# Opening of a fused convolution and SwiGLU kernel: when block 1's x is requested, which queue loads block 0's x, and where pair 1's first group and the third gate bank stand

## The chip, the cores and the metric

The kernel runs on one core of a Trainium2 chip. The metric is device time in microseconds (us), median of several executions. A core has five engines that work side by side, each in its own program order: TensorE (PE, matmuls into PSUM banks), VectorE (DVE), ScalarE (ACT), GpSimd (POOL) and SyncE (SP, which here only issues DMAs and waits). ACT and POOL issue DMAs too. All of them hand their transfers to the same 16 DMA engines.

## The reference

The input x has 8 sequences of 4096 tokens with 192 channels. A causal convolution of 7 taps runs along each sequence; the 192 channels form 8 heads of 24, and the taps are per head, softmaxed over the 7. Its result goes through a SwiGLU feed-forward block with 1536 hidden units.

```
w = softmax(weight)                              # 8 heads x 7 taps
y[b, s, h, :] = sum_k w[h, k] * x_padded[b, s + k, h, :]
g = y @ w_gate;  val = y @ w_val                 # 192 -> 1536
out = (silu(g) * val) @ w_out                    # 1536 -> 192
```

## The kernel before

**Tiling.** The 32768 tokens are cut into 64 blocks of 512 (TB); two blocks make a pair. The 1536 hidden units are cut into 12 chunks of 128 (NCH). The main loop at the end of the kernel runs over blocks and, in each, over chunks; a counter (`at`) numbers the chunks through: 0 to 11 are block 0, 12 to 23 block 1, and chunk 24 begins pair 1. For each chunk PE computes gate and value (`first`, L541 and L542, three steps of two matmuls each, a gate and a value matmul side by side on the two halves of the array), ACT takes silu of the gate (L546), and DVE multiplies it by the value into h (L548). Pieces of the block before's last product (`second`, L553: h times w_out) are put between the chunks from chunk 14 on; ACT evacuates them (L591) and SP stores them (L583).

**PSUM banks.** Two banks hold gates, three hold values, one ("run") belongs to the convolution of the later pairs, and one tile ("acc") to the output. A gate bank is free when silu has read it, a value bank when h is made. In block 0 alone, the chunks named in `PLAN["third"]` take "run" as a third gate bank.

**Convolution of pair 1 and later.** x is loaded by SP in squares of 32 by 32 (`emit_load`, L103, tiles sqA, sqB, and headA, headB for the first pair of a sequence), turned by DVE (`emit_turn`, L114, tiles xtA, xtB), and the taps are split between engines: ACT multiplies tap 0 into "run" (`start_d`, L468) and others into t tiles (L461), DVE adds taps onto "run" (`dve_tap`, L478, the last into aD), POOL multiplies taps (L483), adds the t tiles (L490) and joins all into xc (L496). SP then exchanges the two 64-partition halves into xs (`swapped`, L444 and L445). A pair has three such groups (0, 1, 2; group 1 is the B half). At which chunk each step of a group is put into the program is written by hand in `PLAN`; for pair 1 it is `PLAN["opening"]`, one tuple per group in the order turn, start, ACT taps, DVE taps, POOL taps, join, swap. Steps due at a chunk (`at_chunk`) are put behind that chunk's silu and h.

**Convolution of pair 0.** It is done on PE. `load_x` (L136) brings x of one block into x_sb as six windows of 94 rows. The taps (L132) are turned into a softmaxed band matrix T by small operations on PE, ACT and DVE (L248 to L270), the repeated products (`repeat`, L310) and DVE's cut by a band mask (`cut_band`, L318). For block 0, ACT and POOL cast x to 16 bits (`cast`, L220), PE multiplies by T (`heads`, `convolve`, L331), and the sums are gathered (L380) into the operands D0 to D2. `warm` (L240) are matmuls on zeros that only keep PE occupied. For block 1, POOL casts x by parity into x16p (`cast_parity`, L223), and the product is made between the chunks of block 0: `lateA(0)` behind chunk 2, `lateA(1)` behind chunk 5, `lateC` behind chunk 8. ACT copies the sums (foldA, L660; foldC, L666) and SP exchanges halves (`exchange`, L657: swapA, swapC). Chunk 12 on needs foldA, swapA, foldC and swapC.

**Order of SP's queue before.** Block 0's x (two DMAs); then, behind a wait for block 0's first convolution (`heads(0, 0)`), block 1's x (two DMAs of three windows) and pair 1's sqB; behind `lateA(0)` the first halves of pair 1's sqA; the exchanges for block 1; at chunk 9 the second halves of sqA; group 1's exchange at chunk 13; from then on loads, exchanges, stores and marks (`mark`, L438: an SP no-op that waits for a PE output piece and that a later piece waits for).

**Order of POOL's queue before.** Four iotas, `plain` (L199, L200), the memset of `spread` (L205), the weights of chunks 0 to 3 (`load_w`, L156, a casting DMA each for gate and value), block 0's casts, two copies into `spread` (`place`, L279), the weights of chunks 4 to 7, two more copies, `mask` (L289, L290) and `own` (L297), block 1's casts, the weights of chunks 8 to 11, w_out (L593).

Of the kernel before, what the change touches and what calls it, by code (L numbers as in the profile page):

```python
# [15 lines left out]
    load=((2, -47), (3, -40), (0, -34), (1, -28)),  # L16
    opening=(
# [3 lines left out]
    ),  # L21
    gate=2, val=3, lead=4, third=(2, 8, 11),
)


# [1 line left out]
def kernel(  # L27
# [9 lines left out]
    nc = tc.nc  # L37
    fp32 = mybir.dt.float32
    fp16 = mybir.dt.float16
    int32 = mybir.dt.int32  # L40
    AF = mybir.ActivationFunctionType
    ALU = mybir.AluOpType
    AX = mybir.AxisListType

    B, S, D = x.shape
    H, K = weight.shape
# [4 lines left out]
    grp = D // H  # L51
# [7 lines left out]
    n_pairs = NT // (2 * TB)  # L59
# [3 lines left out]
    const_pool = ctx.enter_context(tc.tile_pool(name="const", bufs=1))  # L63
# [18 lines left out]
    def emit_load(q, part, half=None):  # L82
        head = q % ppb == 0
        if part == 2 and not half:
            squares[q, "A"] = headA if head else xpool.tile(
                [P, HIST + 2 * TB], fp32, tag="sqA", name="sqA"
            )
            squares[q, "B"] = headB if head else xpool.tile(
                [P, HIST + TB], fp32, tag="sqB", name="sqB"
            )  # L90
        for k in range(2):
            quad = 2 * (part % 2) + k
            if part < 2:
                tile_, t0, n, c = squares[q, "A"], 0, 2 * TB, SQ * quad
            else:
                tile_, t0, n, c = squares[q, "B"], TB * (part % 2), TB, P + SQ * k
            skip = HIST if head and t0 == 0 else 0
            row = q * 2 * TB + t0 - HIST + skip
            n = n // SQ + 1 - skip // SQ
            if half is not None:  # L100
                first = TB // SQ + 1
                skip, row, n = ((skip, row, first), (first * SQ, row + first * SQ, n - first))[half]
            nc.sync.dma_start(  # L103
                out=tile_[quad * SQ : (quad + 1) * SQ, skip : skip + n * SQ].rearrange("p (n c) -> p n c", c=SQ),
                in_=x_flat[row : row + n * SQ, c : c + SQ].rearrange("(n p) c -> p n c", p=SQ),
            )
# [9 lines left out]
    def sync_after(ins, earlier, why="one bank, two halves of the array"):  # L116
        tc.add_manual_dep(
            ins.ins,
            earlier.ins.name,
            mybir.DependencyInfo(mybir.DependencyClass.Sync, mybir.DependencyReason.DATA),  # L120
            reason=why,
        )
# [3 lines left out]
    HALF, STEP, W, NW = TB // 2, 85, 88, 6  # L126
# [2 lines left out]
    assert 8 == K + 1 and (NW - 1) * STEP + W > TB and HALF - 3 * STEP in (0, 1)  # L129
    RT = 8 * H  # L130
    taps = const_pool.tile([H, K], fp32, tag="taps", name="taps")
    nc.scalar.dma_start(out=taps, in_=weight)  # L132
    x_sb = xpool.tile([P, 2, NW, D], fp32, tag="x_sb", name="x_sb", bufs=1)

    def load_x(b, lo, hi, skip=0):
        nc.sync.dma_start(  # L136
            out=x_sb[skip:LOADED, b, lo:hi, :],
            in_=bass.AP(
                tensor=x_flat.tensor,
                offset=x_flat.offset + (b * TB + lo * STEP - pad + skip) * D,  # L140
                ap=[[D, LOADED - skip], [STEP * D, hi - lo], [1, D]],
            ),
        )

    load_x(0, 1, NW)
    load_x(0, 0, 1, pad)
    w = wpool.tile([P, 3, Dff], fp16, tag="w_sb", name="w_sb")
    wo_r = wpool.tile([P, NCH, D], fp16, tag="wo_sb", name="wo_sb")
# [5 lines left out]
    def load_w(lo, hi, which):  # L154
        rows, src = w_halves[which]
        nc.gpsimd.dma_start(out=w[rows, :, lo * P : hi * P], in_=src[:, :, lo * P : hi * P])  # L156
# [27 lines left out]
    def where(out, t, bits):  # L184
# [13 lines left out]
    spread = const_pool.tile([P, 4, 2, DB], fp16, tag="spread", name="spread")  # L198
    nc.gpsimd.memset(plain, 0.0)  # L199
    nc.gpsimd.affine_select(  # L200
        out=plain, in_=plain, pattern=[[-32, 4], [-1, grp]],
        compare_op=ALU.not_equal, fill=1.0, base=0, channel_multiplier=1,
    )
    plain = plain[:, :, :].rearrange("p h c -> p (h c)")
    nc.gpsimd.memset(spread, 0.0)  # L205
    load_w(0, 4, 0)
    load_w(0, 4, 1)

    mask = const_pool.tile([RT, D], fp16, tag="mask", name="mask")


    x16 = xpool.tile([P, NW, D + 8], fp16, tag="x16", name="x16", bufs=1)
# [6 lines left out]
    def cast(copy, lo, hi):  # L219
        copy(x16[0:ROWS, lo:hi, 0:D], x_sb[0:ROWS, 0, lo:hi, :])  # L220
# [17 lines left out]
    def warm(n, r=SUBS):  # L238
        for _ in range(n):
            nc.tensor.matmul(  # L240
                early["idle"][:, 0 : r * P].rearrange("p (r c) -> p r c", c=P), zeros,
                zeros.unsqueeze(1).to_broadcast([P, r, P]), start=True, stop=True,
            )

    warm(2)
    warm(1, 3)
    rows = early["D2"][0:RT, 0:K]
    nc.tensor.matmul(rows, whose, taps, start=True, stop=True)  # L248
    nc.vector.tensor_reduce(wmax, rows, axis=AX.X, op=ALU.max, negate=True)
# [20 lines left out]
    nc.vector.tensor_tensor(left[:, 1, :, :], repeated(full), left[:, 0, :, :], op=ALU.subtract)  # L270
    left = left[:, :, :, :].rearrange("r i n m -> r i (n m)")
    nc.scalar.activation(two, one, AF.Silu)
    cast(nc.scalar.copy, 1, 3)
    cast(nc.gpsimd.tensor_copy, 3, NW)
    cast(nc.gpsimd.tensor_copy, 0, 1)

    def place(k):
        lo, hi, at = ((0, DB, 0), (DB, 96, 0), (0, 32, 32), (32, 96, 0))[k]
        nc.gpsimd.tensor_copy(  # L279
            spread[:, k, :, at : at + hi - lo], plain[:, lo:hi].unsqueeze(1).to_broadcast([P, 2, hi - lo])  # L280
        )
# [4 lines left out]
    load_w(4, 8, 1)  # L286
    place(2)
    place(3)
    nc.gpsimd.memset(mask, 0.0)  # L289
    nc.gpsimd.affine_select(  # L290
        out=mask[:, :].rearrange("r (h c) -> r h c", h=H),
        in_=mask[:, :].rearrange("r (h c) -> r h c", h=H),
        pattern=[[-8, H], [0, grp]],
        compare_op=ALU.not_equal, fill=1.0, base=0, channel_multiplier=1,
    )
    own = const_pool.tile([RT, P], fp16, tag="own", name="own")
    nc.gpsimd.tensor_copy(  # L297
        own[:, :].rearrange("h (t c) -> h t c", t=2),
# [9 lines left out]
    def repeat(part, h0):  # L308
        bank = early[("hi", "lo")[part] + "AC"[h0 // HH]]
        return nc.tensor.matmul(  # L310
            bank[0:ROWS, 0 : HH * W], left[:, part, 0:ROWS],
            pick[:, h0 : h0 + HH, :].unsqueeze(2).to_broadcast([RT, HH, W // 8, 8]),
            start=True, stop=True,
        )
# [9 lines left out]
    def convolve(bank, quarters, parts, parities):  # L324

        for part in parts:
            for e in parities:
                for n in range(len(quarters[0])):
                    for a, q in enumerate(quarters):
                        x, h, u0, out = q[n](e)  # L330
                        ins = nc.tensor.matmul(  # L331
                            bank[32 * a : 32 * a + 32, out], x, T[0:ROWS, part, h, u0 : u0 + out.stop - out.start],
                            start=part + e + n == 0, stop=part == 1 and e == parities[-1],
                            skip_group_check=True,
                        )
        return ins

    def piece(win, t0):
        return ends[win] - win * STEP, slice(ends[win] - t0, ends[win + 1] - t0)

    def by_head(h):
        return [
            lambda e, w=w: (x16[0:ROWS, w, grp * h : grp * h + 32], h, *piece(w, 0))
            for w in (3, 4, 5, 0, 1, 2)
        ]

    def by_block(b, half):
# [5 lines left out]
        return [lambda e, w=w: of(e, w) for w in range(half * NW // 2, (half + 1) * NW // 2)]  # L353

    warm(3)
    repeat(0, 0)
    repeat(1, 0)
    repeat(0, HH)
    repeat(1, HH)
# [16 lines left out]
    def heads(k, part):  # L376
        return convolve(sums[k], [by_head(HH * k + a) for a in range(4)], (part,), (0,))
# [3 lines left out]
            early[name], spread[:, k, :, :].rearrange("p t c -> p (t c)"), fold, start=first, stop=last  # L381
        )

    some = heads(0, 0)

    sync_after(nc.sync.nop(), some, "the rest after block 0's x")
    load_x(1, 0, 3)
    load_x(1, 3, NW)
    if n_pairs > 1:
        for part in (2, 3):  # L390
            emit_load(1, part, None)
    heads(0, 1)
    nc.scalar.copy(foldA, sums[0])
    heads(1, 0)
# [13 lines left out]
    raw, rest = (const_pool.tile([RT, K], fp32, tag=n, name=n) for n in ("raw", "rest"))  # L408
# [279 lines left out]
    for q in range(2, n_pairs):  # L688
        base = 2 * NCH * q
        for part, c in PLAN["load"]:  # L690
            c = {2: 14, 3: 16, 0: 18, 1: 21}[part] if q == 2 else base + c
            at_chunk(c, lambda q=q, part=part: emit_load(q, part))
        for g in range(3):
            c = base + PLAN["start"][g]
# [8 lines left out]
    lead = PLAN["lead"]  # L703
# [4 lines left out]
    for n in range(2 * n_pairs):  # L708
        block = Block(n)
# [90 lines left out]
```

## Time and profile before

| | us |
|---|---|
| median of the runs before (lowest to highest) | 778.47 (777.98 to 779.33) |
| the profiled execution | 779.9 |
| its span, first to last instruction | 778.1 |
| PE busy in the span | 766.6 (99%) |
| VectorE, ScalarE, GpSimd busy | 658.5, 662.8, 668.1 |

How to read the lines that follow. In the table of stretches, the columns are the stretch, its length, the busy time of PE, of PE's weight loads, of VectorE, ScalarE and GpSimd with the number of instructions, the clock granted to PE (1.00 is full), the busy share of the DMA engines, and GB/s. In the waits: who waited for whom, the sum in us, how often, the longest. In the timeline: start, duration, engine, line of the kernel, operation, output and inputs, shape, how many instructions were merged, and in square brackets how long the engine stood idle before and what ended it. A "q" behind an engine's name is its instruction queue, where DMAs are issued. A matmul's duration includes its way through the array; the next can start before it ends.

### The profile page before, as it was taken

How to read it: one execution, taken by the hardware profiler on the slowest of the kernel's cores; microseconds unless marked ns; L12 is line 12 of the kernel's file. 1: busy time of each engine (PE TensorE's matmuls, PEld its weight loads, DVE VectorE, ACT ScalarE, POOL GpSimd, SP SyncE). 2: the span in 40 equal slices, each digit the busy share in tenths (PEclk: the TensorE clock that was granted, in tenths of full speed). 3: DMA queues.
4: the chain of work that ended last, by engine and by line, in shares of the span. 5: the costliest groups of instructions: out<-in, count | busy, mean ns of one | idle time of the engine just before them, and what ended most of it. 6: DMA issues, size and time to landing. Idle time of an engine off the chain costs nothing.

```text
span 778.1 us, 28288 instructions
## 1 busy us (share of the span) xinstructions
PE 766.6 (99%) x11035; PEld 626.2 (80%) x11035; DVE 658.5 (85%) x1050; ACT 662.8 (85%) x1188; POOL 668.1 (86%) x651
## 2 busy tenths in 40 slices
PE   7899999999999999999999999999999999999998
PEld 3567777777777777888888888888888888888887
DVE  5688888888888888888888888888888888888875
ACT  4688888888888888888888888888888888888875
POOL 5699988899888899888899888898888898888850
PEclk9999999999999999999999999999999999999999
DMA  7644444334443433443434443434443334343211
GB/s 130 99 90 87 88 90 90 84 88 84 83 99 84 84 89 83 89 98 80 87 86 87 87 97 82 84 84 92 86 90 91 79 83 96 83 94 89 63 46 53
DMA packets 255280, 67.27 MB, mean 86 GB/s; under 512 B 207919, under 2 KB 255145, under 8 KB 255145
## 3 DMA queue, kind: packets, MB, share of 16 engines
q1 hardware_dynamic: 252329, 63.69, 37.9%
q0 software_dynamic: 2800, 1.77, 1.7%
q8 instruction: 86, 1.41, 0.8%
q14 instruction: 49, 0.40, 0.2%
q10 hardware_dynamic: 16, 0.00, 0.0%
HBM read 29.64 MB, written 25.17 MB: 70 GB/s over the span
## 4 chain that ended last, share of the span: by engine, by line
PE 95%; DMA 2%; SPq 1%; ACT 1%; DVE 0%; issue 0%; POOL 0%; DVEq 0%; ACTq 0%; POOLq 0%
PE val L542 45%; PE acc L553 32%; PE gate L541 17%; DMA x_sb<-in_x_dram 1%; SPq L103 1%; DMA xs<-xc 1%; PE idle L240 0%; ACT silu L546 0%; PE acc L751 0%; DMA sqA<-in_x_dram 0%; ACT t L461 0%; POOL x16p L223 0%; SPq L657 0%; PE val L751 0%; PE run L751 0%
## 5 line engine op out<-in xcount | busy, mean ns | idle before, releaser
L548 DVE TENSOR_TENSOR h<-silu,val 128x512 f16<-128x512 f16 x768 | 509.2, 680 | 109.7 <-ACT silu L546 80.9
L546 ACT ACTIVATE silu<-gate 128x512 f16<-128x512 f32 x768 | 453.0, 594 | 87.7 <-PE gate L541 70.5
L553 PE MATMUL acc<-wo_sb,h 64*128 64x192 f16 x6048 | 454.8, 243 | 0.4 <-SPq L438 0.4
L490 POOL TENSOR_TENSOR t<-t,t 128x512 f32<-128x512 f32 x310 | 393.8, 1270 | 62.2 <-ACT t L461 41.3
L553 PEld LDWEIGHTS <-h 64*128 64x128 f16 x6048 | 395.5, 94 | 49.7 <-SPq L438 0.8
L542 PE MATMUL val<-xc,w_sb 64*128 64x512 f16 x1116 | 409.7, 376 | 0.0
L541 PE MATMUL gate<-xc,w_sb 64*128 64x512 f16 x1116 | 409.7, 376 | 0.0
L542 PE MATMUL val<-xs,w_sb 64*128 64x512 f16 x1116 | 360.0, 376 | 0.4 <-DMA xs<-xc 0.4
L541 PE MATMUL gate<-xs,w_sb 64*128 64x512 f16 x1116 | 360.2, 376 | 0.0
L542 PEld LDWEIGHTS <-w_sb 64*128 64x128 f16 x2340 | 212.6, 94 | 80.0 <-issue 4.7
L541 PEld LDWEIGHTS <-w_sb 64*128 64x128 f16 x2340 | 213.0, 94 | 8.8 <-issue 4.8
L496 POOL TENSOR_TENSOR xc<-t,aD 128x512 f16<-128x512 f32 x93 | 118.1, 1270 | 7.3
L483 POOL TENSOR_SCALAR t<-xtA,wn 128x512 f32<-128x512 f32 x155 | 105.9, 694 | 2.7 <-DVE xtA L114 2.7
L461 ACT ACTIVATE t<-xtA,wn 128x512 f32<-128x512 f32 x124 | 88.5, 714 | 0.0
L591 ACT COPY o<-acc 128x384 f32<-128x384 f32 x126 | 60.4, 479 | 16.2 <-DMA sqA<-in_x_dram 4.0
L478 DVE SCALAR_TENSOR_TENSOR aD<-xtA,wn,run 128x512 f32<-128x512 f32 x62 | 46.0, 741 | 0.0
L483 POOL TENSOR_SCALAR t<-xtB,wn 128x512 f32<-128x512 f32 x62 | 42.2, 692 | 3.7 <-DVE xtB L114 3.7
L461 ACT ACTIVATE t<-xtB,wn 128x512 f32<-128x512 f32 x62 | 44.2, 714 | 0.0
L468 ACT ACTIVATE run<-xtA,wn 128x512 f32<-128x512 f32 x62 | 42.6, 686 | 0.8 <-DVE xtA L114 0.8
L114 DVE STREAM_TRANSPOSE xtA<-sqA 128x544 f32<-128x544 f32 (+1 forms) x48 | 34.6, 721 | 0.0
L478 DVE SCALAR_TENSOR_TENSOR run<-xtB,wn,run 128x512 f32<-128x512 f32 x31 | 23.2, 749 | 0.0
L478 DVE SCALAR_TENSOR_TENSOR run<-xtA,wn,run 128x512 f32<-128x512 f32 x31 | 23.2, 749 | 0.0
(111 smaller groups left out, 186.4 us busy)
## 6 DMA issues: line engine op xcount, KB each, us to landing
out_dram<-o SPq DMA_DIRECT2D x127, 192.0 KB, 2.0
sqA<-in_x_dram SPq DMA_DIRECT2D x92, 132.0 KB, 2.8
xs<-xc SPq DMA_DIRECT2D x186, 64.0 KB, 2.0
sqB<-in_x_dram SPq DMA_DIRECT2D x96, 68.0 KB, 2.4
headA<-in_x_dram SPq DMA_DIRECT2D x28, 128.0 KB, 2.5
headB<-in_x_dram SPq DMA_DIRECT2D x14, 68.0 KB, 2.4
headB<-in_x_dram SPq DMA_DIRECT2D x14, 64.0 KB, 2.2
w_sb<-in_moe_w_gate_dram POOLq DMA_DIRECT2D x3, 192.0 KB, 3.8
```

The lines of the kernel that those rows point to most:

```text
L461: mul(parts[-1], *self.tap(k))
L468: nc.scalar.mul(self.aD, *self.tap(0))
L478: nc.vector.scalar_tensor_tensor(out=self.aD, in0=v, scalar=s, in1=run, op0=ALU.mult, op1=ALU.add)
L483: self.product(k, lambda t, v, s: nc.gpsimd.tensor_scalar(t, v, scalar1=s, scalar2=1.0, op0=ALU.mult, op1=ALU.mult), self.parts)
L490: nc.gpsimd.tensor_tensor(self.parts[0], self.parts[0], t, op=ALU.add)
L496: nc.gpsimd.tensor_tensor(xc, self.parts[0], self.aD, op=ALU.add)
L541: nc.tensor.matmul(g, w[0:DB, ca, f], a[0:DB, :], start=(i == 0), stop=(i == 2))
L542: nc.tensor.matmul(v, w[DB:P, cb, f], b[DB:P, :], start=(i == 0), stop=(i == 2))
L546: nc.scalar.activation(s, self.g.pop(j), AF.Silu)
L548: nc.vector.tensor_tensor(h, s, self.v.pop(j), op=ALU.mult)
L553: ins = nc.tensor.matmul(acc, self.h[j][r, ts(s, P)], wo_r[r, j, :], start=first and j == 0, stop=not first and j == NCH - 1, skip_group_c ...
L591: nc.scalar.copy(self.o[:, 2 * half : 2 * half + 2, :], self.acc[:, :, 0:D])
```

## The change

Five things change, all in the opening.

1. The wait that lets SP ask for block 1's x and pair 1's sqB is tied to the first repeated product (`repeat(0, 0)`) instead of to `heads(0, 0)`, and block 1's x is one DMA of six windows instead of two of three.
2. Block 0's x is split over two queues: windows 3 to 5 on ACT's, windows 1 and 2 and then window 0 on SP's. The taps move from ACT's queue to the head of SP's. ACT casts windows 0 and 1, POOL casts 2 to 5 in one instruction, and the products start with window 2.
3. On POOL, the memset of `spread` goes to DVE, and `mask` is made ahead of the first weights instead of behind the second ones.
4. Pair 1's group 1 is put one chunk earlier in all steps but its swap: turn and start at chunk 4, DVE taps at 5 and 6, ACT taps at 6 and 7, POOL's at 6, join at 7.
5. The third gate bank is taken at chunks 2, 9 and 11 instead of 2, 8 and 11.

A warm-up matmul ahead of the taps' product is one column block shorter (2 instead of 3), and one of two column blocks is added ahead of `repeat(0, 0)`.

```diff
     opening=(
         (12, 13, (14, 15), (14, 15), 13, 15, 20),
-        (5, 5, (7, 8), (6, 7), 7, 8, 13),
+        (4, 4, (6, 7), (5, 6), 6, 7, 13),
         (18, 20, (22, 23), (21,), 20, 23, 31),
     ),
-    gate=2, val=3, lead=4, third=(2, 8, 11),
+    gate=2, val=3, lead=4, third=(2, 9, 11),
...
-    nc.scalar.dma_start(out=taps, in_=weight)
+    nc.sync.dma_start(out=taps, in_=weight)
...
-    load_x(0, 1, NW)
+    load_x(0, 3, NW, 0, nc.scalar)
+    load_x(0, 1, 3)
     load_x(0, 0, 1, pad)
...
-    nc.gpsimd.memset(spread, 0.0)
+    nc.vector.memset(spread, 0.0)
+
+    mask = const_pool.tile([RT, D], fp16, tag="mask", name="mask")
+    nc.gpsimd.memset(mask, 0.0)
+    nc.gpsimd.affine_select(
...
     load_w(0, 4, 0)
     load_w(0, 4, 1)
...
     warm(2)
-    warm(1, 3)
+    warm(1, 2)
...
-    cast(nc.scalar.copy, 1, 3)
-    cast(nc.gpsimd.tensor_copy, 3, NW)
-    cast(nc.gpsimd.tensor_copy, 0, 1)
+    cast(nc.scalar.copy, 0, 2)
+    cast(nc.gpsimd.tensor_copy, 2, NW)
...
-            for w in (3, 4, 5, 0, 1, 2)
+            for w in (2, 3, 4, 5, 0, 1)
...
     warm(3)
-    repeat(0, 0)
+    warm(1, 2)
+    some = repeat(0, 0)
+
+    sync_after(nc.sync.nop(), some, "the rest after block 0's x")
+    load_x(1, 0, NW)
+    if n_pairs > 1:
+        for part in (2, 3):
+            emit_load(1, part, None)
     repeat(1, 0)
...
-    some = heads(0, 0)
-
-    sync_after(nc.sync.nop(), some, "the rest after block 0's x")
-    load_x(1, 0, 3)
-    load_x(1, 3, NW)
-    if n_pairs > 1:
-        for part in (2, 3):
-            emit_load(1, part, None)
+    heads(0, 0)
     heads(0, 1)
```

More of the change, by code (lines that the diff above doesn't have):

```diff
@@ L131, with load_x @@
     taps = const_pool.tile([H, K], fp32, tag="taps", name="taps")
-    nc.scalar.dma_start(out=taps, in_=weight)
+    nc.sync.dma_start(out=taps, in_=weight)
     x_sb = xpool.tile([P, 2, NW, D], fp32, tag="x_sb", name="x_sb", bufs=1)
-    def load_x(b, lo, hi, skip=0):
-        nc.sync.dma_start(
+    def load_x(b, lo, hi, skip=0, queue=nc.sync):
+        queue.dma_start(
             out=x_sb[skip:LOADED, b, lo:hi, :],
@@ L204 @@
     plain = plain[:, :, :].rearrange("p h c -> p (h c)")
-    nc.gpsimd.memset(spread, 0.0)
+    nc.vector.memset(spread, 0.0)
+    mask = const_pool.tile([RT, D], fp16, tag="mask", name="mask")
+    nc.gpsimd.memset(mask, 0.0)
+    nc.gpsimd.affine_select(
+        out=mask[:, :].rearrange("r (h c) -> r h c", h=H),
+        in_=mask[:, :].rearrange("r (h c) -> r h c", h=H),
+        pattern=[[-8, H], [0, grp]],
+        compare_op=ALU.not_equal, fill=1.0, base=0, channel_multiplier=1,
+    )
     load_w(0, 4, 0)
     load_w(0, 4, 1)
-    mask = const_pool.tile([RT, D], fp16, tag="mask", name="mask")
     x16 = xpool.tile([P, NW, D + 8], fp16, tag="x16", name="x16", bufs=1)
@@ L288 @@
     place(3)
[L289 to L295, printed above, removed]
     own = const_pool.tile([RT, P], fp16, tag="own", name="own")
```

## The prediction

> **What bounds the kernel now.** I read the page's chain first, then busy time by stretch, then TensorE's waits, then the timeline of the stretch that stands out. All times are us of the profiled execution.
>
> ```profile
> span 778.1 us, 28288 instructions
> PE 95%; DMA 2%; SPq 1%; ACT 1%; DVE 0%; issue 0%; POOL 0%; DVEq 0%; ACTq 0%; POOLq 0%
> ...
> 9.25:16.08 6.83, 3.91 (x77) 1.98 (x78) 3.63 (x11) 2.16 (x4) 2.50 (x5) 1.00 0.68 133
> 16.08:19.49 3.41, 3.41 (x62) 1.47 (x58) 1.47 (x3) 1.79 (x3) 1.05 (x2) 0.50 1.14 166
> 19.49:26.32 6.83, 3.18 (x86) 1.50 (x76) 3.91 (x7) 3.58 (x7) 3.90 (x4) 1.00 0.96 123
> 26.32:29.73 3.41, 3.41 (x20) 1.23 (x18) 1.79 (x3) 2.04 (x4) 2.34 (x2) 0.50 0.23 44
> 29.73:36.56 6.83, 6.65 (x130) 6.13 (x128) 5.48 (x10) 5.73 (x11) 3.96 (x5) 1.00 0.53 89
> 60.00:760.00 700.00, 700.00 (x10024) 580.21 (x10021) 608.24 (x951) 613.69 (x1100) 624.83 (x590) 1.00 0.40 86
> ...
> PE gate L541 <- DVE aD L478: 3.7, 1, 3.7
> PE acc L331 <- POOL x16p L223: 2.9, 2, 2.6
> ```
>
> TensorE (PE) is busy for all 700 us from 60 to 760, and the diff changes nothing there: microseconds saved in the opening stay saved, microseconds lost stay lost, unless a later wait takes them back. Two stretches stand out. From 9.25 to 16.08 PE works 3.91 of 6.83 us, and the next 3.41 us are granted half the clock; from 19.49 to 26.32 it works 3.18 of 6.83, and again 3.41 us at half follow. Each holds one long wait: 2.9 us for block 1's cast x (x16p), and 3.7 us for the last VectorE (DVE) tap of pair 1's first group, because chunk 8 takes the PSUM bank ("run") that this group accumulates in. The change works on both.
>
> **Block 1's x.** The request, the cast and the product that waits for it:
>
> ```profile
> 4.60 0.52 DVE L318 TENSOR_TENSOR T<-hiA,band 94x352 f16<-94x352 f32 x1 [0.25 <-PE hiA L310]
> ...
> 6.44 0.84 SPq L136 DMA_DIRECT2D x_sb<-in_x_dram  x2
> ...
> 11.52 0.17 PE L419 MATMUL acc<-parts,own 64*128 64x21 f16 x1
> 13.58 1.27 POOL L223 CAST x16p<-x_sb 94x576 f16<-94x576 f32 x2 [4.91 <-DMA x_sb<-in_x_dram]
> 14.29 0.30 PE L331 MATMUL acc<-T,x16p 94*32 94x85 f16 x12 [2.60 <-POOL x16p L223]
> 14.90 0.53 PE L331 MATMUL acc<-T,x16p 94*32 94x85 f16 x36 [0.31 <-POOL x16p L223]
> 15.37 0.39 PE L541 MATMUL gate<-D,w_sb 64*128 64x512 f16 x1
> ...
> DMA to landing us min/median/max: 3.6/4.1/6.6
> ```
>
> SyncE's queue (SP) now waits for the first repeated product instead of block 0's first convolution. DVE's wait shows that product ready at 4.6, so the request, one DMA now, leaves at 4.6; the two of before were issued in 0.84 from 6.44. The second took 6.6 us and ended POOL's wait at about 13.5. The x loads took 3.6 to 6.6, so the single load lands between 8.2 and 11.2; I take 9.4, below the middle, because it now starts while only one weight load is still moving. PE can start the product at 11.55. The casts take 0.66 each: the first half is in time for a landing by 10.8, the second by 10.3. At 9.4 the wait is gone; at 11.2 about 0.9 us of it stays. The product then runs 0.6 (36 of its 48 matmuls took 14.90 to 15.37), and chunk 3 starts when h of chunk 0 has freed its value bank (below: 11.45 and 0.68 for one), at **12.17 instead of 15.37: 3.2 us**.
>
> **Chunks 3 to 13, walked by the rows.** Row by row, with an engine's order as in the code:
>
> ```profile
> 10.82 1.57 ACT L546 ACTIVATE silu<-gate 128x512 f16<-128x512 f32 x3 [0.70 <-PE val L542]
> ...
> 11.45 1.88 DVE L548 TENSOR_TENSOR h<-silu,val 128x512 f16<-128x512 f16 x3 [0.42 <-ACT silu L546]
> ...
> 15.60 0.38 PE L541 MATMUL gate<-D,w_sb 64*128 64x512 f16 x1
> ...
> 19.61 0.39 PE L541 MATMUL gate<-D,w_sb 64*128 64x512 f16 x1
> 20.00 0.74 DVE L114 STREAM_TRANSPOSE xtB<-sqB 128x544 f32<-128x544 f32 x1
> 20.84 0.69 ACT L468 ACTIVATE run<-xtB,wn 128x512 f32<-128x512 f32 x1 [0.52 <-DVE xtB L114]
> 21.46 1.06 ACT L546 ACTIVATE silu<-gate 128x512 f16<-128x512 f32 x2
> 23.93 0.74 DVE L478 SCALAR_TENSOR_TENSOR aD<-xtB,wn,run 128x512 f32<-128x512 f32 x1
> 24.73 0.37 PE L541 MATMUL gate<-D,w_sb 64*128 64x512 f16 x1 [3.65 <-DVE aD L478]
> 26.18 0.37 ACT L666 CAST foldC<-acc 128x256 f16<-128x256 f32 x1
> 26.57 1.10 SPq L657 DMA_DIRECT2D swapC<-foldC  x2
> ...
> 30.36 0.27 PE L541 MATMUL gate<-foldA,w_sb 64*128 64x256 f16 x1
> ...
> DMA to landing us min/median/max: 1.7/1.7/1.7
> ```
>
> A chunk is three gate/value pairs 0.22 apart at the full clock (15.37, 15.60), 0.65 in all. Of three silus in 1.57 us each starts 0.49 after the one before, of three h in 1.88 us 0.61.
>
> *Chunks 3 to 5 and the second product:* 3 x 0.65, 0.16 for chunk 5's gate bank, 0.6 for the product: chunk 6 at 14.88, before 19.61. That is 1.5 us more, the first half-clock stretch.
>
> *Chunks 6 to 8:* group 1's transpose is now behind chunk 4's h on DVE: h at 14.28, transpose 14.87 to 15.62, and ScalarE's (ACT) first tap 0.1 later, 15.70 to 16.40. ACT works in order, so chunk 5's silu stands behind that tap (16.32 to 16.91), and chunk 7, which needs chunk 5's gate bank, starts at 16.94. So a **new wait of 1.4 us** opens at 15.53, where 3.7 us were. Then on ACT the fold copy (16.81) and chunk 6's silu (17.30 to 17.90), which frees chunk 8's bank, no longer "run": chunk 8 at 17.93, before 24.73: 2.1 us more.
>
> *Chunks 9 to 13:* chunk 9 takes "run". DVE: h 16.93, tap 17.54, h 18.20, tap 18.81 to 19.55; chunk 9 at 19.6. Chunk 10 at 20.25, chunk 11 behind chunk 9's silu at 21.07, chunk 12 at 21.78. Block 1's C operand is the next one late: its fold copy ends at 20.42 behind the silus, the exchange is issued from 20.45 (two, 0.5 apart) and lands 1.7 after issue, 22.7; chunk 12's second half waits 0.3 to 0.4 for it. Chunk 13 at 22.86, before 30.36: **7.5 us** in all, the second half-clock stretch among them.
>
> **What is late next.**
>
> ```profile
> 30.01 1.97 SPq L444 DMA_DIRECT2D xs<-xc  x1
> ...
> PE acc L553 <- SPq L438: 0.4, 1, 0.4
> ```
>
> From the exchange on, SP's order is as before: x halves, the long 1.97 us issue, more x, then the marks (L438) for which PE's output pieces wait from chunk 16 on, once for 0.4 us already. SP is only 26.57 - 20.45 = 6.1 us early, PE 7.5. So between 0 (a long issue that shrinks, slack in between) and 1.4 us comes back; I charge 0.3, near the 0.4 of that row. **Sum: 7.5 - 0.3 = 7.2 us.** Group 0's transpose follows chunk 12 on DVE and starts POOL's chain, so both move with PE.
>
> **The other edits, taken at nothing.**
>
> ```profile
> 2.02 0.52 POOL L205 MEMSET spread<- 128x512 f16 x1
> ...
> 4.63 0.95 POOL L220 CAST x<-x_sb 94x576 f16<-94x576 f32 x2 [0.65 <-DMA x_sb<-in_x_dram]
> 5.77 0.26 PE L331 MATMUL hiA<-T,x 94*32 94x84 f16 x4
> ...
> 7.60 0.26 POOL L289 MEMSET mask<- 64x192 f16 x1
> 7.93 0.39 POOL L290 TENSOR_SCALAR_AFFINE_SELECT mask<-mask 64x192 f16<-64x192 f16 x1
> ...
> 9.44 0.39 PE L541 MATMUL gate<-D,w_sb 64*128 64x512 f16 x1
> ...
> DMA to landing us min/median/max: 3.4/3.9/6.5
> ```
>
> Block 0's x: the taps go first on SP (one issue, about 0.4 by the row of two in 0.84), x's last windows at once on ACT. The first convolution follows PE's own filler at 5.77, so an earlier x gains nothing. POOL's single cast of four windows is 0.8 long (estimate from 576 columns in 0.66); it is in time for a landing by 4.9, before 4.6. Bounds 0 and 0.5; I take 0. The fillers (0.1 more in all) stand in PE's waits for taps and DVE. POOL: 0.65 of mask for 0.52 of memset ahead of the first weights, 0.1 to 0.2 later. Those weights are issued from 2.02 + 0.52 on, one DMA after the other, and a weight load took 3.9 (6.5 for the slowest), so they land about 7.5 with the delay; chunk 0 needs them at 9.44, and the 1.9 between covers block 1's x beside them. If that cover goes (a 6.5 load), chunk 0 starts 0.6 late. Chunks 4 to 7's weights are issued behind the casts as before and now needed at 12.8, the end of chunk 3, instead of about 16: with the slowest row they are in if issued by 6.3. I take 0; 0.7 if sqB's packets, which now come sooner, crowd them. sqB itself must be in by 14.87, the transpose. Chunks 8 to 11's weights and w_out follow the casts and come 4 us earlier.
>
> **The clock.** Stretches with 57% and 47% of PE busy were followed by half clock, one with 97% was not. By my walk PE idles 1.0 of 6.83 us to 16.08 and about 2.2 of the next 6.83, 68% busy: between the rows. I take the clock as kept, since the longest single wait, 1.4, is well under 2.6 and 3.65. The Trainium skill ("TensorE: Matmul & The Clock Gate", Part 1) says that the clock falls after at least one idle window of about 3.4 us; this trace disagrees, as a wait of 2.6 us was enough. By that rule nothing would fall here, and the sum stays 7.2.
>
> **The rivals.**
> 1. *The clock falls once more*, at about 22.9. For: 68% lies nearer to 57 than to 97. 3.4 us at half clock cost about what the first such stretch did, 1.5 to 1.6 us: gain 5.6.
> 2. *The loads don't come sooner*: they queue behind the weights as the second x load did (6.6). The landing at 11.2 costs 0.9, weights or sqB another 0.7, and a wait over 2 us brings the clock's 1.6: gain about 4.
> 3. *The gain is handed back* in block 1: PE is at 97% from 29.73 only because its inputs were ready; with SP 1.4 us behind, pieces, exchanges and store may slip in turn: gain 1.6 to 4.
> 4. *Slower*: in-order DVE stops at the transpose of chunk 4 until sqB has landed, and h, silu and PE stop behind it, one for one. Before, the transpose at 20.00 waited for no load. It decides from a landing at 22: beyond, all 7.2 us are lost. Against: SP issues sqB right behind x, and no x or w row here took over 6.6 from issue to landing.
>
> **How the numbers follow.** The profiled execution took 779.9 us, 1.8 around its span; the median is 778.47. The gain is taken from the median: forecast 778.47 - 7.2 = **771.3**, chance 0.47 (own range 769.5 to 772.2). Rival 1: 772.9, 0.25. Rival 2: 774.5, 0.12. Rival 3: 774.5 to 776.9, 0.08. No change within 0.2% (1.6 us, about what a measurement here can tell from none): 0.03. Rival 4: over 780, 0.05. Range: below, the forecast without SP's 0.3, with group 1's wait half as long (0.7) and 1.3 of spread between runs (777.98 to 779.33), 769.0; above, 775.0, which takes in rival 2 and leaves about 0.15 out. Faster 0.92, same 0.03, slower 0.05.
>
> **What would show it.** Right: an SP x issue at 4.6 and POOL's cast before 10.3; PE's wait on x16p gone; full clock from 9.25 on; a wait near 1.4 us before chunk 7 that ends in ACT's silu, a small one for swapC; chunk 13 near 22.9; the rest shifted by 7. Wrong: a cast after 11; half clock after 16; PE waiting for aD by over 1 us; waits at L438 or for xs after chunk 13 that were not there.

## The result, and the profile after

The changed kernel takes 773.79 us (median of 4 runs, 773.53 to 775.72), the kernel before 778.66 beside it: ratio 0.9943, 95% interval 0.9924 to 0.9961, or 4.9 us (forecast 7.2). Measured again among the experiments it is 773.82 against 778.98, ratio 0.9938, 0.9923 to 0.9953. The profiled execution took 773.53 against 779.9: 6.4 us. So two gaps have to be explained: 7.2 to 6.4 within the trace, and 6.4 to 4.9 between the trace and the medians. 773.79 lies inside the whole range of the prediction (769.0 to 775.0), but outside the one that it gave for its own walk (769.5 to 772.2).

First the page of the changed kernel, its span and its chain of waits:

```profile
span 771.7 us, 28287 instructions
...
PE 97%; SPq 1%; ACT 1%; issue 0%; DVE 0%; DMA 0%; DVEq 0%; ACTq 0%
```

The same stretches as before, by engine (columns as above):

```profile
9.25:16.08 6.83, 4.95 (x87) 2.49 (x86) 4.15 (x12) 3.28 (x6) 3.53 (x5) 1.00 0.95 137
16.08:19.49 3.41, 2.25 (x64) 1.13 (x61) 2.08 (x5) 1.94 (x5) 1.77 (x3) 1.00 1.39 154
19.49:26.32 6.83, 6.36 (x115) 3.89 (x114) 6.17 (x11) 5.75 (x11) 4.68 (x4) 1.00 0.75 116
26.32:29.73 3.41, 2.93 (x61) 2.42 (x57) 2.65 (x5) 2.90 (x6) 2.74 (x4) 1.00 0.44 81
```

Both half-clock stretches are gone. What PE waits for in the first 100 us of the changed kernel:

```profile
PE acc L331 <- DVE wn L420: 1.8, 1, 1.8
PE gate L541 <- ACT silu L546: 1.2, 1, 1.2
...
PE acc L553 <- SPq L438: 0.4, 1, 0.4
PE gate L541 <- DVE aD L478: 0.3, 1, 0.3
PE D L256 <- DMA taps<-in_weight_dram: 0.2, 1, 0.2
```

The waits of 3.7 for aD and 2.9 for x16p are gone. In their places stand the predicted wait behind ACT (1.2, predicted 1.4) and one that the prediction does not name: 1.8 for wn. The changed kernel's timeline shows how it comes about:

```profile
4.85 0.31 SPq L136 DMA_DIRECT2D x_sb<-in_x_dram  x1
...
11.01 1.27 POOL L231 CAST x16p<-x_sb 94x576 f16<-94x576 f32 x2 [3.31 <-DMA x_sb<-in_x_dram]
...
11.43 1.88 DVE L548 TENSOR_TENSOR h<-silu,val 128x512 f16<-128x512 f16 x3 [0.42 <-ACT silu L546]
11.47 0.17 PE L419 MATMUL acc<-parts,mask 64*128 64x21 f16 x1
...
13.23 0.19 DVE L420 TENSOR_REDUCE wn<-acc 128x14 f32<-128x42 f32 x1
13.48 0.65 PE L331 MATMUL acc<-T,x16p 94*32 94x85 f16 x48 [1.81 <-DVE wn L420]
...
16.79 0.74 DVE L114 STREAM_TRANSPOSE xtB<-sqB 128x544 f32<-128x544 f32 x1
...
17.62 0.69 ACT L468 ACTIVATE run<-xtB,wn 128x512 f32<-128x512 f32 x1 [1.47 <-DVE xtB L114]
18.25 0.58 ACT L546 ACTIVATE silu<-gate 128x512 f16<-128x512 f32 x1
18.88 0.37 PE L541 MATMUL gate<-D,w_sb 64*128 64x512 f16 x1 [1.16 <-ACT silu L546]
...
19.33 1.16 SPq L657 DMA_DIRECT2D swapA<-foldA  x2
...
19.85 0.37 PE L541 MATMUL gate<-D,w_sb 64*128 64x512 f16 x1
...
20.72 0.74 DVE L478 SCALAR_TENSOR_TENSOR aD<-xtB,wn,run 128x512 f32<-128x512 f32 x1
...
23.65 0.27 PE L541 MATMUL gate<-foldA,w_sb 64*128 64x256 f16 x1
...
24.14 0.27 PE L541 MATMUL gate<-swapA,w_sb 64*128 64x256 f16 x1
...
24.77 0.28 PE L541 MATMUL gate<-foldA,w_sb 64*128 64x256 f16 x1
```

Behind chunk 2, `lateA(0)` first spreads the taps: two small matmuls (L419, 11.47) into the tile "acc", which DVE reduces to wn (L420). The second product writes the same tile, so it waits for the reduction; the reduction stands on DVE behind the three h of chunks 0 to 2 (11.43 to 13.31) and ends at 13.42. Block 1's x is not what PE waits for here, though POOL's first cast starts only at 11.01: a sign that the prediction had named as wrong (before 10.3 was right, after 11 wrong). Its one load, by the view of tile x_sb in the changed kernel:

```profile
DMA to landing us min/median/max: 6.1/6.1/6.1
```

The predicted starts of the chunks beside the measured ones (us from the span's start):

| chunk | before | predicted | after | after less predicted |
|---|---|---|---|---|
| 3 | 15.37 | 12.17 | 14.05 | 1.9 |
| 6 | 19.61 | 14.88 | 16.89 | 2.0 |
| 7 | 20.26 | 16.94 | 18.88 | 1.9 |
| 8 | 24.73 | 17.93 | 19.85 | 1.9 |
| 9 | 26.06 | 19.6 | 21.51 | 1.9 |
| 12 | 29.66 | 21.78 | 23.65 | 1.9 |
| 13 | 30.36 | 22.86 | 24.77 | 1.9 |

From chunk 3 on the walk held to 0.1; its start was 1.9 late, and 5.6 of the 7.5 are there at chunk 13. A second thing is late at the same place. The exchange of A is asked for at 19.33, and its landing, by the view of tile swapA in the changed kernel, takes 4.4 to 4.8. The prediction priced only C's exchange, at 1.7:

```profile
DMA to landing us min/median/max: 4.4/4.6/4.8
```

Chunk 12's second half starts on swapA at 24.14. Whether the lateness of chunk 3 cost anything that this exchange would not have cost anyway was the first question for the experiments.

### The profile page after: what moved, and what is told of

Read it like the earlier page. It is cut to its first block, busy times and chain, and to the rows that moved or that the text cites. A ratio compares the mean times of both kernels' runs of the same rounds, so it can differ in the third digit from the quotient of the medians.

```text
span 771.7 us, 28287 instructions
## 1 busy us (share of the span) xinstructions
PE 763.6 (99%) x11036; PEld 673.4 (87%) x11036; DVE 658.4 (85%) x1051; ACT 663.2 (86%) x1188; POOL 667.9 (87%) x649
## 4 chain that ended last, share of the span: by engine, by line
PE 97%; SPq 1%; ACT 1%; issue 0%; DVE 0%; DMA 0%; DVEq 0%; ACTq 0%
PE val L542 41%; PE acc L553 30%; PE gate L541 24%; SPq L103 0%; ACT silu L546 0%; PE acc L751 0%; PE idle L248 0%; SPq L444 0%; DMA taps<-in_weight_dram 0%; PE D L387 0%; DVE h L548 0%; SPq L657 0%; PE val L751 0%; PE run L751 0%; PE hiA L331 0%
## 5 line engine op out<-in xcount | busy, mean ns | idle before, releaser
L553 PE MATMUL acc<-wo_sb,h 64*128 64x192 f16 x6048 | 435.9, 243 | 0.4 <-SPq L438 0.4
```

The source lines that it names most:

```text
L553: ins = nc.tensor.matmul(acc, self.h[j][r, ts(s, P)], wo_r[r, j, :], start=first and j == 0, stop=not first and j == NCH - 1, skip_group_c ...
```

## The experiments

They ran in three sets of four, each set on one chip beside the kernel before; the changed kernel itself is in the second set. Chunk starts, landings and stretches of half clock given without a row are read from the traces of these runs.

**The request alone.** The kernel before with SP's wait tied to the first repeated product and block 1's x in one DMA; nothing else.

```diff
-    some = heads(0, 0)
...
+    some = repeat(0, 0)
+    sync_after(nc.sync.nop(), some, "the rest after block 0's x")
+    load_x(1, 0, NW)
```

> Before with part 1 alone: SP's wait moved to the first repeated product, block 1's x in one DMA. Theory (waits ahead of chunk 3 and the clock): x lands near 10.9 as in the changed kernel, but the second product still starts only at 13.4 to 13.5, behind DVE's sum of the tap parts, so chunk 3 is 1.3 us early, the first half-clock stretch is gone (another 1.5), and the wait for the run bank before chunk 8 stays at 3.5 to 3.9 us: 2.3 to 3.0 us faster than before. Rival (the run bank ends last): what is early at chunk 3 is waited out before chunk 8: that wait grows to 5 us or more and the time is within 0.8 us of before.

Measured: 777.51 against 778.85, ratio 0.9989 (0.9978 to 0.9999): 1.3 faster by the medians, between theory and rival; the interval reaches from 0.1 to 1.7. x was asked for at 4.59 and landed 5.1 later, so the loads do come sooner. PE's waits in this kernel (its lines are one lower):

```profile
PE gate L540 <- DVE aD L477: 4.0, 1, 4.0
PE acc L331 <- DVE wn L419: 1.7, 1, 1.7
```

The wait for wn is here without any other part of the change: it belongs to the order of the program before, where x16p came later still and hid it. Chunk 3 starts at 14.35, one us earlier than before instead of the 3.2 of the walk.

**Group 1 and the third bank alone.** The kernel before with the two edits of `PLAN`.

```diff
-        (5, 5, (7, 8), (6, 7), 7, 8, 13),
+        (4, 4, (6, 7), (5, 6), 6, 7, 13),
-    gate=2, val=3, lead=4, third=(2, 8, 11),
+    gate=2, val=3, lead=4, third=(2, 9, 11),
```

> Before with parts 4 and 5 alone: group 1 a chunk earlier, third gate bank at 2, 9 and 11. Theory: the wait of 2.9 us for block 1's cast x and the half-clock stretch behind it stay as they were; the wait for the run bank falls from 3.7 to under 0.5 and one near 1.3 before chunk 7 takes its place: 2.0 to 3.0 us faster. Rival (the late x sets everything): group 1's turn now waits for chunk 4 at half clock and the gain is under 1 us.

Measured: 776.21, ratio 0.9966 (0.9955 to 0.9977): 2.6 faster, as expected, and the largest single part. Its profile has the two expected waits, 0.3 for aD and 1.2 behind ACT. The wait of 2.9 for x16p, which the theory kept, isn't there: in this execution the full clock came only at 10.87, the first chunks were later, and the product waits 1.8 for wn and 0.3 for x16p.

**Both together.**

```diff
+    some = repeat(0, 0)
...
+        (4, 4, (6, 7), (5, 6), 6, 7, 13),
+    gate=2, val=3, lead=4, third=(2, 9, 11),
```

> Parts 1, 4 and 5 without parts 2 and 3 (block 0's x in two queues, taps on SP, spread and mask moved, fillers). Theory: these edits are worth nothing, so this kernel is within 0.5 us of the changed one, about 773.5 to 774.3; the first repeated product is 0.2 to 0.3 us earlier here, as the added filler is not there. Rival: the two queues or the earlier mask carry a part of the gain, then this one is 1 us or more slower than the changed kernel.

Measured: 775.31, ratio 0.9953 (0.9939 to 0.9967): 3.5 faster, near the sum of 1.3 and 2.6, but 1.5 slower than the changed kernel: the theory missed, and the rival fits. The mean clock of the single executions tells what both are needed for: it is 0.999 or more in none of 11 with the request alone, in 3 of 12 with the plan alone, in all 5 with both.

**The product ahead of the taps.** The changed kernel, with the second product issued before the taps are spread, so that it no longer waits for DVE.

```diff
-            spread_taps(late["sum"][:, 1, :])
         ins = halves(g, late["sum"][:, g, :])
+        if g == 0:
+            spread_taps(late["sum"][:, 1, :])
```

> The changed kernel with the tap spreading (two small matmuls and DVE's sum, wn) put behind the second product instead of ahead of it. Theory: PE's wait of 1.8 us for that sum goes, the product starts with the cast at 11.7 and ends near 12.9, but chunk 4 is then held by its value weights, which land at 14.2, so only about 0.5 us of 1.8 comes out: 773.2. Rival (nothing else is late): chunk 3 and all behind it move by 1.1 to 1.4 us: about 772.5.

Measured: 773.36, ratio 0.9932 (0.9917 to 0.9947). The wait for wn is gone, chunk 3 starts at 13.15 and chunk 12 at 22.84 (0.8 earlier than in the changed kernel), yet chunk 13 starts at 24.76, as there. In this kernel's waits of PE stands what took its place:

```profile
PE gate L541 <- DMA swapA<-foldA: 0.7, 1, 0.7
```

So the wait for wn, though it is the longest, is worth some 0.4 us by the medians (773.36 against 773.79 and 773.82), and by the intervals, which overlap, perhaps nothing: the exchange holds chunk 12 either way. The time is near the theory's 773.2, but the reason is another: chunk 4's weights, which it named, take little, since the lead at chunk 12 is still 0.8.

**The changed kernel again**, with no edit, as a base for the next three.

> The changed kernel itself, beside the three runs that follow, to have all of them against one set of runs of before. If the two theories of the forecast's miss hold (the profiled execution of before had two half-clock stretches where its median run has one, worth some 1.2; TensorE's wait of 1.8 for DVE's first tap gives about 0.5 in the end), the time is 773.3 to 774.2, gain 4.7 to 5.5. Rival: the first measurement of the change was a lucky one; then 774.5 or more.

Measured: 773.82, ratio 0.9938 (0.9923 to 0.9953), as expected. Its profile holds something new. PE's timeline in this execution:

```profile
6.79 0.59 PE L387 MATMUL D<-foldA,spread 128*128 128x512 f16 x2
7.72 0.59 PE L387 MATMUL D<-foldC,spread 128*128 128x512 f16 x2 [0.35 <-POOL own L297]
8.25 0.39 PE L541 MATMUL gate<-D,w_sb 64*128 64x512 f16 x1
```

Chunk 0 starts 1.07 earlier than in the first profile of the same kernel (9.32), where the first of these pairs took 1.03 instead of 0.59. But the span is only 0.2 shorter. By the starts of the silus the lead is 1.3 at the 17th and 0.2 at the 37th; PE's waits in this execution name the marks on SP:

```profile
PE acc L553 <- SPq L438: 1.3, 2, 0.8
```

Rival 3's mechanism is there, then: what PE wins ahead of chunk 13 is in part given back to SP's queue.

**The fillers alone added** to the kernel with both parts, and **the fillers alone taken out** of the changed kernel: two kernels, one question, what the edits costed at nothing are worth.

```diff
-    warm(1, 3)
+    warm(1, 2)
...
     warm(3)
+    warm(1, 2)
     some = repeat(0, 0)
```

> The request and both plan edits (775.31, with 1.4 to 1.6 more than the whole change) plus the two filler edits alone: one column block less ahead of the taps' product, two more ahead of the first repeated product. Theory: the two queues for block 0's x and POOL's moved mask carry the missing 1 us or so, since they bring chunk 0 forward; the fillers are worth under 0.3: 775.0 to 775.6. Rival: the fillers set when the clock is granted and carry it: 773.9 to 774.5.

> The changed kernel without its two filler edits. Theory: same as the changed kernel within 0.4 (773.4 to 774.2), full clock from about 9. Rival (fillers carry 1 us): 774.6 to 775.4, with the first full clock or chunk 0 later by 0.5 or more.

Measured: with them 774.75 (0.9950, 0.9937 to 0.9964), between theory and rival; without them 774.05 (0.9939, 0.9925 to 0.9953), as expected. On the same chip the changed kernel took 773.82. The fillers are worth 0.2, which is within the spread, where everything else is in place; the other edits (two queues for block 0's x, the taps on SP, the mask) about 0.9, though the intervals overlap. Taking them at nothing was an error of under 1 us, in the change's favour.

**w_out asked for later.** The kernel with the product first, and w_out's load on POOL behind chunk 6 instead of behind the weights.

```diff
-    nc.gpsimd.dma_start(out=wo_r, in_=moe_w_out.rearrange("(c p) d -> p c d", p=P))
...
+    at_chunk(6, lambda: nc.gpsimd.dma_start(out=wo_r, in_=moe_w_out.rearrange("(c p) d -> p c d", p=P)))
```

> The changed kernel with the second product ahead of the wait for DVE's first tap (the kernel that took 773.36), and with w_out asked for by POOL behind chunk 6 instead of in the opening. Theory: behind chunk 11 the floor is block 1's exchanges, which are slow because w_out's transfer shares the DMA engines; without it swapA lands by 22 instead of 24.0 to 24.4, chunk 12's second half starts 0.7 to 1.2 earlier, time 772.2 to 772.7. Rival: the exchanges land when ACT's fold copies and SP's queue let them, w_out beside them or not: gain under 0.3, 773.1 to 773.6; or POOL's issue comes too late for the first output pieces, 774 or more with a wait for w_out.

Measured: 777.54, ratio 0.9983 (0.9972 to 0.9994), 4 slower than without this edit. The theory's mechanism held and its time did not. From issue to landing in this kernel, first by the view of tile swapA, then by that of swapC:

```profile
DMA to landing us min/median/max: 2.0/2.0/2.0
```

```profile
DMA to landing us min/median/max: 5.1/5.3/5.5
```

w_out is now asked for at 19.01 and lands at 26.26. swapA, before it, takes 2.0 instead of the 5.3 to 5.5 it took beside w_out in the kernel with the product first; swapC, now beside it, takes 5.1 to 5.5 instead of 2.7 to 3.1 in the kernel with the product first, where it met w_out's end, and 1.9 to 2.1 in the changed kernel. The wait moved to the other exchange, and a wait of this length takes the clock. In this kernel's waits and stretches:

```profile
PE gate L541 <- DMA swapC<-foldC: 3.3, 1, 3.3
```

```profile
26.32:29.73 3.41, 3.25 (x33) 2.79 (x34) 1.97 (x3) 1.97 (x4) 0.77 (x2) 0.51 0.40 75
```

So w_out's transfer is what holds block 1's exchanges. The trace's records of packets show how: swapC, asked for at 20.99 and 21.49, began its first of 128 packets at 24.60, when 1377 of w_out's 1536 had begun; in the changed kernel swapA's first began at 20.52, when 1348 had. The Trainium skill ("DMA: Bandwidth & Descriptors", Queues, rings and completion order) says that a DMA engine takes turns between its queues, a packet at a time. Equal turns, one record each, are not what this trace shows; whether a record is what the page calls a packet, no run here shows.

**The first wait filled.** The kernel before, with nine matmuls on zeros in PE's wait for x16p.

```diff
             spread_taps(late["sum"][:, 1, :])
+            for _ in range(9):
+                nc.tensor.matmul(
+                    late["sum"][:, 0, :].rearrange("p (r c) -> p r c", c=P), zeros,
+                    zeros.unsqueeze(1).to_broadcast([P, SUBS, P]), start=True, stop=True,
+                )
```

> The kernel before with nine matmuls on zeros put ahead of the second repeated product, in TensorE's wait of 2.9 for block 1's x; none of the change is in it. Theory: the half-clock stretch that follows the first wait goes and nothing else, worth what the executions of before with one such stretch and with two lie apart (median 778.56 of 20 against 779.6 of 18): 0.8 to 1.2 faster, 777.6 to 778.1, fewer executions with two stretches. Rival: the clock has no part in the median, or the added matmuls delay the product: within 0.3 of before, or slower.

Measured: 780.06 against 778.96, ratio 1.0013 (1.0002 to 1.0023): slower, as the rival has it; the theory missed. PE's waits and two of the stretches:

```profile
PE gate L541 <- DVE aD L478: 4.0, 1, 4.0
PE acc L650 <- DVE wn L420: 1.8, 1, 1.8
```

```profile
16.08:19.49 3.41, 3.38 (x84) 1.64 (x74) 1.74 (x3) 2.22 (x4) 1.39 (x2) 1.00 0.95 127
...
26.32:29.73 3.41, 3.41 (x48) 1.40 (x38) 1.38 (x2) 1.97 (x5) 1.61 (x2) 0.51 0.08 20
```

The added matmuls write the same tile, so they themselves waited for wn and ended too late: chunk 3 starts at 16.11, 0.74 after that of before. The first half-clock stretch did go, but the wait of 4.0 was then followed by half clock from 22.84 to 29.67. The run doesn't price a stretch; it shows again that the wait for wn is in the kernel before.

**The third bank back at chunk 8**, in the changed kernel.

```diff
-    gate=2, val=3, lead=4, third=(2, 9, 11),
+    gate=2, val=3, lead=4, third=(2, 8, 11),
```

> The changed kernel with the third gate bank taken at chunks 2, 8 and 11 as before. Theory: chunk 8 then waits for the last VectorE tap of pair 1's first group (ready at 21.5 where chunk 8 starts at 19.85), 1.5 later, and chunk 9, whose bank is now an ordinary one, makes up a part: 0.8 to 1.5 slower, 774.6 to 775.3. Rival: the exchanges at 24.1 to 24.7 hold chunk 12 either way: within 0.3 of the changed kernel.

Measured: 776.43 against 778.96, ratio 0.9963 (0.9951 to 0.9976): 2.5 of the gain of 4.9 to 5.2 are left, so that some 2.5 go, more than the 0.8 to 1.5 expected. PE's waits in its profile:

```profile
PE acc L331 <- POOL x16p L231: 2.9, 2, 2.5
PE gate L541 <- DVE aD L478: 1.8, 1, 1.8
```

The wait for aD is 1.8 instead of 0.3, the 1.5 of the theory. The rest above it has another cause in this execution: x landed at 12.38, and half clock followed from 14.75 to 18.16. Three of the five executions have a mean clock below 0.999; the two that kept it took 775.03, inside the theory's range, and 775.89, 0.6 above it.

**The marks early.** The kernel with the product first, with pair 2's loads two, one and one chunks later, behind SP's first marks.

```diff
-            c = {2: 14, 3: 16, 0: 18, 1: 21}[part] if q == 2 else base + c
+            c = {2: 16, 3: 17, 0: 19, 1: 21}[part] if q == 2 else base + c
```

> The kernel with the second product ahead of the wait for DVE's first tap (773.36), and pair 2's loads asked for at chunks 16, 17, 19 and 21 instead of 14, 16, 18 and 21, so that SyncE's first marks stand ahead of four more DMA issues. Theory: from chunk 14 on SyncE's queue is the bound (an execution of the changed kernel whose chunk 0 came 1.1 earlier was 0.9 ahead at silu 16 and 0.2 at silu 36, with 1.3 of wait for the marks), so TensorE's waits for marks go and 0.4 to 1.0 is won: 772.4 to 773.0. Rival: the marks come only from the long issue that moves with the queue, or the later loads are late for pair 2's turn: 773.2 or more.

Measured: 773.92, ratio 0.9935 (0.9919 to 0.9951). Its six times fall into two sets, 772.64 to 772.76 and 775.08 to 775.92, so that the median says nothing. PE has no wait for marks in this profile, and the 17th to 37th silu lie 20.2 apart (21.6 in the repeat of the changed kernel, but 20.6 in its first profile). That fits the theory and doesn't show it: two profiles without this edit (the filled wait, w_out later) have no wait for marks either, and the next run, which has the edit, has one of 0.4. What it is worth stays open. The profile is one of the second set; block 1's x, by the view of tile x_sb, and PE's first wait:

```profile
DMA to landing us min/median/max: 8.3/8.3/8.3
```

```profile
PE acc L331 <- POOL x16p L231: 3.4, 2, 3.1
```

**The squares later.** The kernel of the last run, with pair 1's sqB asked for behind block 0's first convolution again.

```diff
     load_x(1, 0, NW)
-    if n_pairs > 1:
-        for part in (2, 3):
-            emit_load(1, part, None)
...
-    heads(0, 0)
+    some = heads(0, 0)
+    if n_pairs > 1:
+        sync_after(nc.sync.nop(), some, "squares after block 0's product")
+        for part in (2, 3):
+            emit_load(1, part, None)
```

> The kernel of the run before this one, and pair 1's sqB asked for behind block 0's first convolution again, as in the kernel before, with block 1's x still asked for at the first product. Theory: x and the weights of chunks 4 to 7 share the DMA engines with sqB in the changed kernel; without it x lands by 10 instead of 10.5 to 11.2 and the last of those weights by 13.4 instead of 14.1, w_out and block 1's exchanges 0.3 to 0.7 sooner: 0.3 to 0.6 faster than the run before this one. Rival: sqB then lands after the transpose's place (16.8), VectorE stands, and it is 0.3 or more slower; or the floor lies elsewhere and nothing changes by over 0.3.

Measured: 773.19 against 778.96, ratio 0.9918 (0.9905 to 0.9930), the lowest of all. But its reason failed. The weights came sooner (13.28); x did not (tile x_sb):

```profile
DMA to landing us min/median/max: 8.1/8.1/8.1
```

So asking for sqB later, here at 6.45 instead of 5.21, does not bring x sooner. The interval overlaps that of the changed kernel (0.9923 to 0.9953), so that this version beats it isn't shown.

## Why the prediction was right, and where it wasn't

**Right.** The direction and the order of size; which two waits go; the wait of 1.4 behind ACT's tap (1.2); the third bank's wait for aD (0.3); no stall of DVE at the transpose, rival 4 (sqB landed by 14.65, transpose at 16.79); the distances from chunk 3 to 13, all within 0.1. The clock was kept in 9 of the 10 executions of the changed kernel (0.999 or 1.0; 0.997 in one, as in rival 1). The walk's longest wait of 1.4 was taken to be harmless; measured, 1.8 was too. The runs narrow this further: behind single waits of 1.2 to 1.8 no profile shows half clock, behind those of 2.5, 2.6, 2.8, 3.1, 3.3, 3.7 and 4.0 each does. The Trainium skill ("TensorE: Matmul & The Clock Gate", Part 1) names an idle window of about 3.4 us as the condition; here 2.5 was enough.

**Luck.** That 773.79 lies in the whole range is in part luck. Its upper end was set to take in rival 2, loads that come no sooner; what cost the time was a wait, an exchange and a median that no rival names, and they happened to cost less than rival 2's price.

**Wrong: "PE can start the product at 11.55" and "At 9.4 the wait is gone".** The walk looked at x16p alone. PE's product also waits for DVE's wn, because both use "acc". The trace of before shows no such wait, since x16p ended last there, but the program's order gives it, and DVE's row in that trace has wn ready only at 13.45:

```profile
13.25 0.20 DVE L420 TENSOR_REDUCE wn<-acc 128x14 f32<-128x42 f32 x1
```

This wait ended last and made chunk 3 1.9 late. The load was mis-sized too, hidden behind it: it took 6.1, not 4.8. In the kernel with the product first, chunk 3 starts 1.85 behind POOL's first cast (13.15 and 11.30); by the same distance the changed kernel's cast at 11.01 gives 12.86 (an estimate), so about 0.7 of the 1.9 would stay without the wait for wn. Where x landed at 9.89 and the product came first (w_out later), chunk 3 starts at 12.24, the walk's 12.17. There PE then meets a term that the walk took at nothing, chunk 4's weights, and chunk 12 starts at 22.36, 0.6 behind the walk:

```profile
13.61 0.39 PE L542 MATMUL val<-D,w_sb 64*128 64x512 f16 x1 [0.35 <-DMA w_sb<-in_moe_w_val_dram]
```

**Wrong: "Block 1's C operand is the next one late".** Only C's exchange was priced, by a row from a moment without w_out; it took 1.9 to 2.1 for the 1.7. A's took 4.4 to 4.8 beside w_out's transfer, which runs until 23.71. The price was in the trace of before, by the view of tile swapA there:

```profile
DMA to landing us min/median/max: 4.3/4.5/4.7
```

With the wait for wn taken away, A's exchange holds chunk 13 where it was (product first: 24.76 against 24.77). And with A's exchange in time, the wait for wn keeps chunk 12 at 23.65; its last matmul then waits for C's exchange, which moves with PE, and chunk 13 starts 1.1 later (22.58 and 23.68 in the repeat, with 0.3 of wait for swapC). Either of the two alone keeps chunk 13 near 24.8; of the 1.9, the load's 0.7 would stay without both.

**Wrong in sign, small: the 0.3 charged for SP, and the edits at nothing.** From chunk 13 to the end the gain grew from 5.6 to 6.4: before's wait of 0.4 for xs did not come, and another 0.4 I have not traced. The edits taken at nothing bring up to 0.9.

**Wrong: "The gain is taken from the median."** The sum was made in an execution of 779.9 with two half-clock stretches and subtracted from a median of 778.47. Of 57 executions of before in the three sets, 29 have a mean clock of 0.997 or 0.998 (median 778.46), 25 of 0.995 or 0.996 (median 779.81) and three of 0.993. The profiled one, with 0.995 and two stretches, is of the second sort; a profile with one stretch has 0.998 (the request alone). The walk won back both stretches, while by these clocks the executions have about one and a half on average. The sum: 7.2 forecast, less 1.9, plus 0.3 and 0.8, is 6.4; less 1.24 (profiled execution of before above its median of 778.66) and 0.26 (that of after below its own) is 4.9.

Left open: the worth of a half-clock stretch by an experiment of its own (the filled wait failed); why x's tail is sometimes late (below); the worth of the marks.

## What to carry to other kernels

When an edit takes away the wait that ended last, list every semaphore that the waiting instruction has, by the tiles it writes as well as those it reads: a shorter wait that was hidden takes its place, and behind that there is often a transfer with a landing time of its own. Price a transfer by a row in which the same other transfers run beside it. And take a gain from the execution in which it was worked out: if its clock isn't that of the median run, what it wins back from the clock isn't all to be had.

## What was not expected of the hardware

**A load's tail.** Block 1's x, one DMA of 432 KB asked for at 4.5 to 5.0, landed at 9.69, 9.89, 10.09, 10.51, 10.53, 10.95, 11.24, 12.38, 12.55, 12.76 and 12.81 in the eleven profiles that have it. It isn't slow as a whole: of its 576 packets, 559 had begun by 9.0 in the changed kernel and 536 in the run with the squares later, but in the latter the last 13 began between 11 and 12. Three of the four late ones were followed by half clock. No run here shows what holds these packets.

**The first full clock.** In 5 of the 14 profiles chunk 0 starts at 8.15 to 8.44, in the others at 9.3 to 9.7, and the changed kernel itself has both, 9.32 and 8.25. In the five the full clock was granted between 4.12 and 4.71, in the others that record it between 8.73 and 10.87. The first matmuls on spread take 0.59 a pair in the repeat of the changed kernel and 1.03 in its first profile. The Trainium skill ("TensorE: Matmul & The Clock Gate", Part 1) says that the window is free-running and the cold span varies between runs; the two profiles of the changed kernel agree. Little of their 1.1 reaches the end (0.2), as SP's marks show.
